# Query copies of VectorE between its scales, and a new order of the first units, in an attention and GEGLU kernel

## The chip, the cores and the metric

The kernel runs on one core of a Trainium2 chip. The metric is the device time of one execution in microseconds (us). Several executions of a kernel are taken beside executions of the kernel before on the same chip; one of them is taken with a profile. The time is about 2 us longer than the span of the profile.

## The reference

Linear attention with cosine weights, then a gated feed-forward block over its output. Eight batches of 576 tokens, eight heads of 64, model width 512, inner width 1536.

```python
def phi(x, c, s):
    r = np.maximum(x, 0.0)
    return np.concatenate([r * c, r * s], axis=-1)
q_p, k_p = phi(q, cos_w, sin_w), phi(k, cos_w, sin_w)
kv = np.einsum('bhsf,bhsd->bhfd', k_p, v);  z = np.sum(k_p, axis=2)
num = np.einsum('bhsf,bhfd->bhsd', q_p, kv)
den = np.einsum('bhsf,bhf->bhs', q_p, z)[..., None] + 1e-06
x = (num / den).transpose(0, 2, 1, 3).reshape(B * S, H * D)
g = x @ w_gate
return (0.5 * g * (1 + erf(g / sqrt(2))) * (x @ w_val)) @ w_out
```

## The kernel before

Only the prologue matters: all that happens before the feed-forward units of the first block run one behind the other. It has two chains that meet in the first unit.

- *Attention.* VectorE and ScalarE scale the keys and queries of batch 0 (`sk`, `sq`), TensorE turns (transposes) the queries (`q_by_pe`) into PSUM, the buffer `ps` that its results go to, and a copy brings them to SBUF, the main on-chip memory (`q_evac`), TensorE makes the kv products (`kv_half`) and the numerators (`numer_mm`), VectorE normalises (`norm`), TensorE turns the result, a copy puts it into `xT` (`x_by_pe`). The 576 tokens are five column tiles x0 to x4 (the last is 64 wide).
- *Weights.* `load_w(j0, j1)` lets GpSimd issue two DMAs, one of gate and one of value weights, that cast from fp32 to bf16. A one-element ScalarE copy that reads the end of `qf` holds the first of them back until the queries have landed.

A feed-forward unit is four gate matmuls, a Gelu on ScalarE, four value matmuls and a product on VectorE. Its arguments are block, weight column, first token, width, gate bank and value bank (a bank is one of the slots of `ps`, its second index; a unit that re-uses a bank has to wait until the bank has been read):

```python
def gv_unit(n, jt, c0, w, gb, vb, mid=()):
    p0 = starts[n] + c0
    for ct in range(CT):
        nc.tensor.matmul(ps[:, gb, 0:w], lhsT=wg_sb[:, ct, jt*128:(jt+1)*128],
                         rhs=xT[:, ct, p0:p0+w], start=(ct == 0), stop=(ct == CT-1))
    gel = rot.tile([128, 512], FP32, name="gel", bufs=3)
    nc.scalar.activation(gel[:, 0:w], ps[:, gb, 0:w], AF.Gelu)
    for f in mid:
        f()
    for ct in range(CT):
        nc.tensor.matmul(ps[:, vb, 0:w], lhsT=wv_sb[:, ct, jt*128:(jt+1)*128], ...)
    nc.vector.tensor_mul(hT[n % 2][:, jt, 64+c0:64+c0+w], gel[:, 0:w], ps[:, vb, 0:w])
```

The prologue (cuts marked):

```python
dummies(22)                     # junk matmuls, meant to warm TensorE's clock
...                             # scales of the keys
for h0 in (0, 4):
    if h0:
        nc.scalar.copy(wg_sb[0:1, 0, 0:1], qf[0:1, 7, NJ, D - 1:D])
        load_w(0, 2)
    for j in range(NJ + 1):
        sq(j, 0, "v", h0, h0 + 4)
        sq(j, 1, "v" if j < 2 else "s", h0, h0 + 4)
    for j in range(NJ):
        q_by_pe(0, j, j, None, h0, h0 + 4)
    dummies(2, 7)
q_evac(0, 0, 0, "s")
cast_v(0, 0, 2, "v"); cast_v(0, 2, 4, "s")
load_w(2, 4)
kv_half(0, 0, 4, None)
cast_v(0, 4, 6, "v"); cast_v(0, 6, 8, "s")
q_evac(0, 1, 1, "v")
...                             # kv, numerators and turn of x0, x1
gv_unit(0, 0, 0, 128, 0, 1);   gv_unit(0, 1, 0, 128, 5, 4)      # tile 0
x_by_pe(0, 1, x1, 0, "s");     x2 = numer(0, 2, 6)
gv_unit(0, 0, 128, 128, 5, 1); gv_unit(0, 1, 128, 128, 0, 4)    # tile 1
q_evac(0, 3, 3, "v");          q_by_pe(0, 4, 2, "s")
x_by_pe(0, 2, x2, 5, "s");     x3 = numer(0, 3, 6)
gv_unit(0, 0, 256, 128, 0, 1); gv_unit(0, 1, 256, 128, 3, 4)
x_by_pe(0, 3, x3, 5, "s");     x4 = numer(0, 4, 6)
gv_unit(0, 2, *A, 0, 1);       gv_unit(0, 3, *A, 3, 4)          # A = (0, 256)
x_by_pe(0, 4, x4, 5, "v")
gv_unit(0, 2, *Bw, 0, 1);      gv_unit(0, 3, *Bw, 3, 4)         # Bw = (256, 320)
gv_unit(0, 0, 384, 192, 0, 1); gv_unit(0, 1, 384, 192, 3, 4)
...
for jt in range(4, 11):         # "the regular units"
    gv_unit(0, jt, *A, 0, 3);  gv_unit(0, jt, *Bw, 1, 2)
```

I call everything up to the first tile's units *the front* and what follows, up to the regular units, *the back*.

## Time and profile before

| | before |
|---|---|
| time, median of 3 runs | 334.81 us (334.25 to 334.89) |
| span of the profile | 332.7 us |
| first gate matmuls / first value matmuls | 18.32 / 19.13 us |
| second tile's gate matmuls | 20.87 us |
| regular units start | 31.66 us |
| from there to the end | 301.0 us |

The page of the kernel before: busy time of the engines with their share of the span, and two rows of its 40 slices in tenths.

```profile
PE 321.7 (97%) x2260; PEld 171.5 (52%) x2260; DVE 177.2 (53%) x394; ACT 149.9 (45%) x275; POOL 21.5 (6%) x39
...
PE   7879999999999999999999999999999999999995
...
PEclk9799999999999999999999999999999999999999
```

TensorE has gaps in the first three slices and at the end only. So the start of the regular units is the number to watch: what the prologue saves, the kernel saves.

The chain of waits of the same profile over the prologue (start, length, what):

```profile
4.88 5.52 DMA qf<-in_q_dram
...
10.92 2.56 POOL wg_sb L292
13.48 5.60 DMA wv_sb<-in_moe_w_val_dram
...
19.13 0.40 PE ps L222 x4
```

The timeline of the same profile, cut to GpSimd's weight issues, some of VectorE's work beside them, and TensorE's milestones (start, length, engine, line, operation; in brackets the idle time before and what ended it):

```profile
10.92 2.57 POOL L292 DMA_DIRECT2D wg_sb<-in_moe_w_gate_dram  x1 [8.20 <-ACT wg_sb L345]
...
11.97 0.87 DVE L132 TENSOR_SCALAR qp<-qf,cos_c 128x256 bf16<-128x256 f32 x3
...
12.76 0.55 DVE L138 CAST vx<-vf 128x640 bf16<-128x640 f32 x1
...
13.48 0.90 POOL L293 DMA_DIRECT2D wv_sb<-in_moe_w_val_dram  x1
...
13.66 0.56 DVE L138 CAST vx<-vf 128x640 bf16<-128x640 f32 x1 [0.35 <-DMA vf<-in_v_dram]
...
18.32 0.64 PE L213 MATMUL ps<-xT,wg_sb 128*128 128x128 bf16 x4
...
19.13 0.40 PE L222 MATMUL ps<-xT,wv_sb 128*128 128x128 bf16 x4 [0.17 <-DMA wv_sb<-in_moe_w_val_dram]
...
20.87 0.38 PE L213 MATMUL ps<-xT,wg_sb 128*128 128x128 bf16 x4 [0.42 <-ACT xT L327]
...
28.15 0.72 PE L213 MATMUL ps<-xT,wg_sb 128*128 128x320 bf16 x4 [0.70 <-DVE xT L329]
...
31.66 0.60 PE L213 MATMUL ps<-xT,wg_sb 128*128 128x256 bf16 x4
```

The first weight issue took 2.57 us; it ended in the first pause of VectorE, between two casts at 13.31 and 13.66. The value weights landed at 19.08, and 0.17 us of TensorE's idle time is put down to them.

### The profile page before, as it was taken

Reading aid. Unit: us, or ns where it says so; the run is one execution under the profiler, and the core shown is the slowest. Engines: PE = TensorE matmul, PEld = TensorE weight load, DVE = VectorE, ACT = ScalarE, POOL = GpSimd, SP = SyncE. Lnnn points to the kernel's source line nnn. Section 1 sums busy time; section 2 is a strip of 40 time slices with the busy share of each in tenths; the row PEclk is TensorE's granted clock in tenths of the full one; section 3 lists DMA queues with packets and bytes.
Section 4 is the critical chain, followed back from the end, with each engine's and each line's share of the span. In section 5 each row is a group of like instructions: output and inputs, shape, how many; then the busy total and the mean of one; then the engine's idle time right before and its main releaser. Section 6 shows DMA issues by size and latency. Waiting matters only on the chain.

```text
span 332.7 us, 5946 instructions
## 1 busy us (share of the span) xinstructions
PE 321.7 (97%) x2260; PEld 171.5 (52%) x2260; DVE 177.2 (53%) x394; ACT 149.9 (45%) x275; POOL 21.5 (6%) x39
## 2 busy tenths in 40 slices
PE   7879999999999999999999999999999999999995
PEld 2567766765445444544454445544454444444443
DVE  5775468776674548454755576457635323222210
ACT  6764468783473237422742265325532322322321
POOL 2550010000100001000100010001000100000000
PEclk9799999999999999999999999999999999999999
DMA  7899998999388965994499439992925121000024
GB/s 239 229 166 206 242 340 264 310 226 359 66 112 231 349 102 95 249 323 119 86 253 333 110 75 203 375 142 54 184 47 76 21 63 34 32 32 33 33 64 95
DMA packets 84380, 54.65 MB, mean 164 GB/s; under 512 B 49408, under 2 KB 79872, under 8 KB 84352
## 3 DMA queue, kind: packets, MB, share of 16 engines
q1 hardware_dynamic: 78128, 49.10, 59.2%
q0 software_dynamic: 5792, 4.72, 9.2%
q10 hardware_dynamic: 432, 0.46, 0.4%
q8 instruction: 17, 0.28, 0.3%
q14 instruction: 11, 0.09, 0.1%
HBM read 37.75 MB, written 9.44 MB: 142 GB/s over the span
## 4 chain that ended last, share of the span: by engine, by line
PE 86%; DVE 4%; DMA 3%; ACT 2%; issue 2%; POOL 1%; SPq 1%; DVEq 0%; POOLq 0%; ACTq 0%
PE ps L245 27%; PE ps L213 26%; PE ps L222 26%; PE ps L167 3%; DVE vx L138 3%; PE ps L151 2%; DMA wv_sb<-in_moe_w_val_dram 2%; DMA qf<-in_q_dram 2%; PE ps L311 1%; PE ps L264 1%; ACT kp L134 1%; POOL wg_sb L292 1%; SPq L78 1%; ACT xT L327 1%; DVE hT L226 0%
## 5 line engine op out<-in xcount | busy, mean ns | idle before, releaser
L226 DVE TENSOR_TENSOR hT<-gel,ps 128x512 bf16<-128x512 f32 (+4 forms) x128 | 77.1, 603 | 130.4 <-PE ps L222 127.5
L213 PE MATMUL ps<-xT,wg_sb 128*128 128x512 bf16 (+5 forms) x512 | 114.4, 346 | 2.1 <-ACT xT L327 1.2
L222 PE MATMUL ps<-xT,wv_sb 128*128 128x512 bf16 (+5 forms) x512 | 114.3, 346 | 0.2 <-DMA wv_sb<-in_moe_w_val_dram 0.2
L218 ACT ACTIVATE gel<-ps 128x512 f32<-128x512 f32 (+4 forms) x128 | 67.8, 531 | 85.1 <-PE ps L213 83.7
L245 PE MATMUL ps<-wo_sb,hT 128*128 128x512 bf16 x420 | 96.2, 379 | 0.0
L222 PEld LDWEIGHTS <-wv_sb 128*128 128x128 bf16 x512 | 48.8, 98 | 45.5 <-DMA wv_sb<-in_moe_w_val_dram 0.3
L213 PEld LDWEIGHTS <-wg_sb 128*128 128x128 bf16 x512 | 46.8, 98 | 41.9 <-issue 2.1
L245 PEld LDWEIGHTS <-hT 128*128 128x128 bf16 x420 | 40.2, 98 | 45.8
L275 ACT COPY o_sb<-ps 128x512 f32<-128x512 f32 x35 | 20.5, 586 | 75.5 <-PE ps L245 72.4
L182 DVE TENSOR_TENSOR xb<-ps,rec 128x512 bf16<-128x512 f32 (+1 forms) x41 | 27.8, 678 | 1.5
L134 ACT ACTIVATE kp<-kf,sin_c 128x512 bf16<-128x512 f32 (+1 forms) x41 | 25.3, 679 | 0.7 <-DMA kf<-in_k_dram 0.7
L132 DVE TENSOR_SCALAR qp<-qf,cos_c 128x512 bf16<-128x512 f32 (+1 forms) x45 | 21.0, 510 | 0.7 <-DMA qf<-in_q_dram 0.7
L167 PEld LDWEIGHTS <-qT 128*128 128x128 bf16 x320 | 15.1, 98 | 9.1 <-issue 1.8
L134 ACT ACTIVATE qp<-qf,sin_c 128x512 bf16<-128x512 f32 (+1 forms) x30 | 18.8, 670 | 0.3 <-DMA qf<-in_q_dram 0.3
L132 DVE TENSOR_SCALAR kp<-kf,cos_c 128x512 bf16<-128x512 f32 (+1 forms) x45 | 18.0, 451 | 1.0 <-DMA kf<-in_k_dram 1.0
L167 PE MATMUL ps<-kv,qT 128*128 128x65 bf16 x320 | 16.8, 193 | 0.6 <-DVE qT L317 0.4
L206 POOL COPY xT<-xr 128x256 bf16<-128x256 bf16 x6 | 2.4, 401 | 205.2 <-DMA xr<-xb 205.2
L151 PEld LDWEIGHTS <-kp 128*128 128x128 bf16 x320 | 11.5, 99 | 3.8 <-issue 2.9
L151 PE MATMUL ps<-vx,kp 128*128 128x65 bf16 x320 | 12.2, 195 | 0.5
L138 DVE CAST vx<-vf 128x1280 bf16<-128x1280 f32 (+1 forms) x14 | 12.1, 892 | 0.3 <-DMA vf<-in_v_dram 0.3
L124 PE MATMUL ps<-junk 128*128 128x512 bf16 x32 | 10.0, 450 | 1.7 <-DVE par_i L101 1.7
L231 POOL COPY hT<-hT 128x768 bf16<-128x768 bf16 x8 | 7.6, 946 | 39.5 <-DVE hT L226 39.5
(53 smaller groups left out, 93.9 us busy)
## 6 DMA issues: line engine op xcount, KB each, us to landing
out_dram<-o_sb SPq DMA_DIRECT2D x38, 128.0 KB, 2.4
qf<-in_q_dram SPq DMA_DIRECT2D x7, 640.0 KB, 6.1
kf<-in_k_dram SPq DMA_DIRECT2D x7, 640.0 KB, 8.1
out_dram<-o_sb SPq DMA_DIRECT2D x16, 256.0 KB, 3.0
vf<-in_v_dram SPq DMA_DIRECT2D x6, 640.0 KB, 9.7
qf<-in_q_dram SPq DMA_DIRECT2D x7, 512.0 KB, 4.8
kf<-in_k_dram SPq DMA_DIRECT2D x7, 512.0 KB, 6.7
vf<-in_v_dram SPq DMA_DIRECT2D x6, 512.0 KB, 8.4
```

Source lines behind the costliest of these rows:

```text
L132: nc.vector.tensor_scalar(d, s, col, 0.0, op0=ALU.mult, op1=ALU.max)
L134: nc.scalar.activation(d, s, AF.Relu, scale=col)
L138: cp(vx[b % 2][:, :, h0:h1, 0:D], vf[:, h0:h1].rearrange("p h j d -> p j h d"))
L151: nc.tensor.matmul(ps[:, bank, (h % 4) * (D + 1):(h % 4 + 1) * (D + 1)], lhsT=kp[:, j, h, :], rhs=vx[b % 2][:, j, h, 0:D + 1], start=(j == ...
L167: nc.tensor.matmul(ps[:, bank + g, (h % 4) * (D + 1):(h % 4 + 1) * (D + 1)], lhsT=qT[b % 2][:, t, h, :], rhs=kv[b % 2][:, h, 0:D + 1], sta ...
L182: nc.vector.tensor_tensor(xb[:, g0:g1], nd[:, :, :, 0:D], rec[:, 0:n, :, None].to_broadcast([128, n, 4, D]), op=ALU.mult,)
L213: nc.tensor.matmul(ps[:, gb, 0:w], lhsT=wg_sb[:, ct, jt * 128:(jt + 1) * 128], rhs=xT[:, ct, p0:p0 + w], start=(ct == 0), stop=(ct == CT - 1),
L218: nc.scalar.activation(gel[:, 0:w], ps[:, gb, 0:w], AF.Gelu)
L222: nc.tensor.matmul(ps[:, vb, 0:w], lhsT=wv_sb[:, ct, jt * 128:(jt + 1) * 128], rhs=xT[:, ct, p0:p0 + w], start=(ct == 0), stop=(ct == CT - 1),
L226: nc.vector.tensor_mul(hT[n % 2][:, jt, 64 + c0:64 + c0 + w], gel[:, 0:w], ps[:, vb, 0:w])
L245: nc.tensor.matmul(ps[:, bank, :], lhsT=hT[n % 2][:, jt, c0:c0 + 128], rhs=wo_sb[:, jt, :], start=(jt == 0), stop=(jt == JT - 1),)
L275: nc.scalar.copy(o_sb, ps[:, bank, :])
```

## The change

Its intent: VectorE copies query turns out of PSUM *between* its scales, so that GpSimd gets to issue the weights; copies, turns and units follow the order in which their inputs arrive; the 192-wide pair of units is split into 128 and 64, so that its first part need not wait for x4. Core of the diff:

```diff
-    dummies(22)
+    dummies(30)
     ...  # scales of the keys as before, then those of the queries' first half (a4), turned
-    (gate of the loads, load_w(0, 2), second half's scales, its turns, dummies(2, 7))
-    q_evac(0, 0, 0, "s")
-    cast_v(0, 0, 2, "v")
-    cast_v(0, 2, 4, "s")
+    nc.scalar.copy(wg_sb[0:1, 0, 0:1], qf[0:1, 7, NJ, D - 1:D])
+    load_w(0, 2)
     load_w(2, 4)
+    q_evac(0, 0, 0, "v", *a4)
+    sq(0, 0, "v", *b4), sq(0, 1, "s", *b4)
+    sq(1, 0, "v", *b4), sq(1, 1, "v", *b4)
+    q_evac(0, 1, 1, "v", *a4)
+    for j in range(2, NJ + 1):
+        sq(j, 0, "v", *b4), sq(j, 1, "s", *b4)
+    ...  # turns of the second half, dummies(1, 7)
+    cast_v(0, 0, 4, "s")
     kv_half(0, 0, 4, None)
     cast_v(0, 4, 6, "v")
     cast_v(0, 6, 8, "s")
-    q_evac(0, 1, 1, "v")
+    q_evac(0, 0, 0, "v", *b4)
+    q_evac(0, 1, 1, "v", *b4)
     ...
     gv_unit(0, 0, 0, 128, 0, 1)
     gv_unit(0, 1, 0, 128, 5, 4)
     x_by_pe(0, 1, x1, 0, "s")
+    q_evac(0, 3, 3, "s", *a4)
     x2 = numer(0, 2, 6)
     gv_unit(0, 0, 128, 128, 5, 1)
     gv_unit(0, 1, 128, 128, 0, 4)
-    q_evac(0, 3, 3, "v")
-    q_by_pe(0, 4, 2, "s")
-    x_by_pe(0, 2, x2, 5, "s")
+    q_evac(0, 3, 3, "s", *b4)
+    x_by_pe(0, 2, x2, 2, "v")
     x3 = numer(0, 3, 6)
-    gv_unit(0, 0, 256, 128, 0, 1)
-    gv_unit(0, 1, 256, 128, 3, 4)
-    x_by_pe(0, 3, x3, 5, "s")
+    gv_unit(0, 2, *A, 5, 1)
+    q_by_pe(0, 4, 3, "s")
+    gv_unit(0, 3, *A, 0, 4)
+    x_by_pe(0, 3, x3, 2, "s")
     x4 = numer(0, 4, 6)
-    gv_unit(0, 2, *A, 0, 1)
-    gv_unit(0, 3, *A, 3, 4)
-    x_by_pe(0, 4, x4, 5, "v")
-    gv_unit(0, 2, *Bw, 0, 1)
-    gv_unit(0, 3, *Bw, 3, 4)
-    gv_unit(0, 0, 384, 192, 0, 1)
-    gv_unit(0, 1, 384, 192, 3, 4)
+    gv_unit(0, 0, 256, 128, 5, 1)
+    gv_unit(0, 1, 256, 128, 0, 4)
+    gv_unit(0, 0, 384, 128, 5, 1)
+    gv_unit(0, 1, 384, 128, 0, 4)
+    x_by_pe(0, 4, x4, 3, "v")
+    gv_unit(0, 2, *Bw, 5, 1)
+    gv_unit(0, 3, *Bw, 0, 4)
+    gv_unit(0, 0, 512, 64, 5, 1)
+    gv_unit(0, 1, 512, 64, 0, 4)
```

More of the change, by code (lines that the diff above doesn't have):

```diff
@@ L335, in sk @@
         scale(K, j, which, eng, *h)
-    dummies(22)
+    a4, b4 = (0, 4), (4, 8)
+    dummies(30)
     for h0 in (0, 4):
@@ L342 @@
             sk(j, 1, "v" if j < 2 else "s", h0, h0 + 4)
-    for h0 in (0, 4):
-        if h0:
-            nc.scalar.copy(wg_sb[0:1, 0, 0:1], qf[0:1, 7, NJ, D - 1:D])
-            load_w(0, 2)
-        for j in range(NJ + 1):
-            sq(j, 0, "v", h0, h0 + 4)
-            sq(j, 1, "v" if j < 2 else "s", h0, h0 + 4)
-        for j in range(NJ):
-            q_by_pe(0, j, j, None, h0, h0 + 4)
-        dummies(2, 7)
-    q_evac(0, 0, 0, "s")
-    cast_v(0, 0, 2, "v")
-    cast_v(0, 2, 4, "s")
-    load_w(2, 4)
+    for j in range(NJ + 1):
+        sq(j, 0, "v", *a4)
+        sq(j, 1, "v" if j < 2 else "s", *a4)
+    for j in range(NJ):
+        q_by_pe(0, j, j, None, *a4)
+    dummies(1, 7)
+    nc.scalar.copy(wg_sb[0:1, 0, 0:1], qf[0:1, 7, NJ, D - 1:D])
+    load_w(0, 2)
+    load_w(2, 4)
+    q_evac(0, 0, 0, "v", *a4)
[4 more added lines that the diff above has]
+        sq(j, 0, "v", *b4), sq(j, 1, "s", *b4)
+    for j in range(NJ):
+        q_by_pe(0, j, j, None, *b4)
+    dummies(1, 7)
+    cast_v(0, 0, 4, "s")
     kv_half(0, 0, 4, None)
@@ L366 @@
     norm(x0, 6, 0, 1)
-    dummies(2, 4)
+    dummies(1, 4)
     numer_mm(0, 0, 6, 1)
     norm(x0, 6, 1, 2)
-    q_evac(0, 2, 2, "s", 0, 4)
+    q_evac(0, 2, 2, "s", *a4)
     dummies(1, 5)
@@ L375 @@
     x1 = numer(0, 1, 6)
-    q_evac(0, 2, 2, "s", 4, 8)
+    q_evac(0, 2, 2, "s", *b4)
     nc.gpsimd.tensor_copy(tiny[0:1, 1:2], x0[0:1, 1, 3, D - 1:D])
```

## The prediction

> **What bounds the kernel now.** TensorE is busy 97% of the 332.7 us span (busy table). After about 31.7 us it has practically no gaps: the windows view gives 268 us busy of 272 between 60 and 332. So only the prologue is left, and the change touches only that. The chain of waits over it: query load to 10.40; a one-element ScalarE gate; GpSimd's issue of the first weight load, 10.92 to 13.48; the first value weights' DMA, landing 19.08; then matmuls broken by waits until 28.15. The regular units (jt = 4) start at 31.66. From 18.3 to 31.66 TensorE is busy 11.04 of 13.36 us: about 2.3 us of gaps, at 19.0, 20.2 to 20.9, 22.6 to 24.0 and 27.4 to 28.15 (timeline).
>
> **The weight issue.** The first GpSimd issue took 2.57 us, later ones 0.75 to 0.76. It ended at 13.48, just after VectorE's unbroken run of scales and a cast (to 13.31). The Trainium skill ("SBUF — State Buffer", the warning on DVE blocking SWDGE DMAs) says that GpSimd can't write descriptors while VectorE runs a 2-port fp32 SBUF operation; this trace agrees (2.57 against 0.75 us). A copy out of PSUM isn't such an operation. The change puts two PSUM query copies of VectorE (half of the 0.68 us for 1024 elements, about 0.4 each) among the second half's scales, at about 10.9 and 12.0. I expect the first issue to end by 11.7 to 12.3 and the second by about 13.4 (before 14.38), so the value weights land about 1 us earlier, near 18.1.
>
> **The attention chain.** This gains less. The first x tile was in SBUF at 18.63, only 0.45 before the weights. The change takes the 1.01 us copy off ScalarE and gives it a cast of about 1.3 us before the first kv product; the second half's scales end 0.4 to 0.5 later on VectorE. Dummies rise from 22 to 30, filling the gap from 8.1 to 9.75 after which the granted clock fell to 0.5 (12 to 14 us); a warmer clock would save some tenths in turns and kv matmuls. I estimate the first x tile at 18.1 to 18.3. The first units, now not waiting for weights, start about 0.5 us earlier.
>
> **The new order.** It moves query copies of tile 3 to ScalarE in halves before they are needed, the x turn of tile 2 to VectorE (0.4 instead of 0.59), and two 256-wide units (0.88 us each, needing only tiles 0 and 1) into the old gap at 22.6 to 24.0. It splits a 192-wide pair into 128 and 64. The total of matmul work is nearly unchanged. New waits are likely: at the fourth tile's units VectorE is in a 1.1 us normalisation, so PSUM comes free late (about 0.6 us), and the 320-wide units still wait for x4 (about 0.6 us). I put the regular units at about 30.7 instead of 31.66.
>
> **Total.** Gain 0.9 us, all on the critical path, since TensorE is full afterwards; the later loads shift with the weight stream. Predicted 333.9 us, 8 in 10 between 333.1 and 334.7; within 2% almost surely.
>
> **What would show it.** First weight issue under 1.5 us; value weights landed near 18; first gate unit near 18 with its value matmuls following directly; no gap over 0.5 us between 22 and 24; jt = 4 gate matmuls starting at 30.2 to 31.2; nothing changed in length after that.
>
> **What would make it wrong.** Scales leaving GpSimd starved between the two copies; earlier weight traffic delaying the value loads (kv product late); the clock throttling later, on real matmuls instead of on turns; the new VectorE order holding up the x4 turn so that all gain is returned before 31 us. Or all the gaps close, and the gain is 2 us.

## The result, and the profile after

The changed kernel took 334.74 us (median of 4 runs, 334.50 to 335.33) beside 334.53 us of the kernel before (4 runs, 333.85 to 334.89). The ratio is 1.0011, with a 95% interval from 0.9988 to 1.0034. A ratio is the mean time of one kernel's runs over that of the other's in the same rounds, so it isn't quite the ratio of the medians. The change shows no gain here, and the median lies just above the predicted range.

The timeline of the changed kernel, cut in the same way:

```profile
11.08 0.42 DVE L317 COPY qT<-ps 128x512 bf16<-128x512 bf16 x1
...
11.18 0.90 POOL L292 DMA_DIRECT2D wg_sb<-in_moe_w_gate_dram  x1 [8.46 <-ACT wg_sb L350]
...
12.07 0.76 POOL L293 DMA_DIRECT2D wv_sb<-in_moe_w_val_dram  x1
...
17.71 0.64 PE L213 MATMUL ps<-xT,wg_sb 128*128 128x128 bf16 x4
...
18.18 0.39 PE L222 MATMUL ps<-xT,wv_sb 128*128 128x128 bf16 x4
...
20.16 0.38 PE L213 MATMUL ps<-xT,wg_sb 128*128 128x128 bf16 x4 [0.42 <-ACT xT L327]
...
21.84 0.30 PE L167 MATMUL ps<-kv,qT 128*128 128x65 bf16 x4 [0.27 <-ACT qT L317]
...
26.61 0.38 PE L222 MATMUL ps<-xT,wv_sb 128*128 128x128 bf16 x4 [0.49 <-DVE hT L226]
...
28.24 0.72 PE L213 MATMUL ps<-xT,wg_sb 128*128 128x320 bf16 x4 [0.58 <-DVE xT L329]
...
31.23 0.28 PE L222 MATMUL ps<-xT,wv_sb 128*128 128x64 bf16 x4 [0.30 <-DVE hT L226]
31.35 0.60 PE L213 MATMUL ps<-xT,wg_sb 128*128 128x256 bf16 x4
```

The front did what was hoped: the first issue takes 0.90 us, the value weights land at 16.7 (12.07 plus 4.6, the DMA view's time to landing), the first value matmuls wait for nothing and start 0.95 us earlier, the second tile's gate matmuls 0.71 us earlier. But the regular units start only 0.31 us earlier. From the second tile's gate to the regular units the back takes 11.19 us, where before it took 10.79. Three waits stand out: at 26.61 and 31.23 for products of VectorE, and at 28.24 for VectorE's copy of x4. Only the first two are new in kind: the old back waits for x4's copy too, 0.70 us at 28.15. A smaller wait, at 21.84, is for a query copy. From 31.35 to the end it is 301.0 us, as before.

VectorE's timeline in that stretch:

```profile
24.83 0.42 DVE L226 TENSOR_TENSOR hT<-gel,ps 128x256 bf16<-128x256 f32 x1 [1.19 <-ACT gel L218]
25.16 0.16 DVE L179 TENSOR_SCALAR den<-ps 128x8 f32<-128x8 f32 x1
...
25.66 0.69 DVE L182 TENSOR_TENSOR xb<-ps,rec 128x512 bf16<-128x512 f32 x1
26.27 0.47 DVE L226 TENSOR_TENSOR hT<-gel,ps 128x128 bf16<-128x128 f32 x2
...
27.76 0.42 DVE L329 COPY xT<-ps 128x256 bf16<-128x256 bf16 x1
```

VectorE waited 1.19 us for a Gelu that stood behind a 1.01 us query copy on ScalarE. It then normalised x4, and only then made the products of tile 2, which free the PSUM banks of the next two units. It copied x4 last.

### The profile page after: what moved, and what is told of

Its sections match the earlier page's. It is cut to its first block, busy times and chain, and to the rows that moved or that the text cites. A ratio compares the mean times of both kernels' runs of the same rounds, so it can differ in the third digit from the quotient of the medians.

```text
span 332.4 us, 6000 instructions
## 1 busy us (share of the span) xinstructions
PE 322.4 (97%) x2281; PEld 171.3 (52%) x2281; DVE 177.2 (53%) x397; ACT 150.3 (45%) x278; POOL 19.7 (6%) x39
## 4 chain that ended last, share of the span: by engine, by line
PE 89%; DVE 5%; ACT 2%; issue 1%; DMA 1%; DVEq 0%; ACTq 0%
PE ps L245 27%; PE ps L213 26%; PE ps L222 26%; PE ps L167 3%; PE ps L124 3%; DVE vx L138 3%; PE ps L151 2%; PE ps L311 1%; PE ps L264 1%; ACT kp L134 1%; DMA out_dram<-o_sb 1%; DVE hT L226 1%; PE ps L325 1%; ACT gel L218 0%; DVE xb L182 0%
## 5 line engine op out<-in xcount | busy, mean ns | idle before, releaser
L226 DVE TENSOR_TENSOR hT<-gel,ps 128x512 bf16<-128x512 f32 (+5 forms) x130 | 77.0, 596 | 131.3 <-PE ps L222 128.1
L218 ACT ACTIVATE gel<-ps 128x512 f32<-128x512 f32 (+5 forms) x130 | 68.2, 525 | 84.7 <-PE ps L213 83.4
L275 ACT COPY o_sb<-ps 128x512 f32<-128x512 f32 x35 | 20.5, 585 | 75.9 <-PE ps L245 72.8
L124 PE MATMUL ps<-junk 128*128 128x512 bf16 x37 | 11.4, 451 | 1.7 <-DVE par_i L101 1.7
L138 DVE CAST vx<-vf 128x1280 bf16<-128x1280 f32 (+1 forms) x13 | 11.7, 934 | 0.3 <-DMA vf<-in_v_dram 0.3
```

The lines of the kernel that those rows point to most:

```text
L124: nc.tensor.matmul(ps[:, bank, :], lhsT=junk[:, 0:128], rhs=junk, start=True, stop=True)
L138: cp(vx[b % 2][:, :, h0:h1, 0:D], vf[:, h0:h1].rearrange("p h j d -> p j h d"))
L226: nc.vector.tensor_mul(hT[n % 2][:, jt, 64 + c0:64 + c0 + w], gel[:, 0:w], ps[:, vb, 0:w])
```

## The experiments

Two questions. Where did the front's gain go (theory T1: to the fourth tile in the new back)? And what does the front really gain? The second came up after the first experiments, when the kernel before showed two kinds of runs.

All traces in one table. "Gate" and "value" are the first gate and value matmuls, "tile 1" the second tile's gate matmuls, "regular" the regular units; "back" is regular minus tile 1. The time is that of the profiled run.

| run | front | back's order | time | gate | value | tile 1 | regular | back |
|---|---|---|---|---|---|---|---|---|
| before | old | old | 334.75 | 18.32 | 19.13 | 20.87 | 31.66 | 10.79 |
| after | new | new | 334.50 | 17.71 | 18.18 | 20.16 | 31.35 | 11.19 |
| e0_again | new | new | 334.65 | 17.93 | 18.41 | 20.39 | 31.57 | 11.18 |
| e1_front | new | old | 334.58 | 18.28 | 18.76 | 20.74 | 31.53 | 10.79 |
| e2_back | old | new | 335.37 | 17.29 | 19.37 | 21.11 | 32.30 | 11.19 |
| e3_banks | new | new, banks | 333.95 | 18.29 | 18.76 | 20.74 | 30.86 | 10.12 |
| e4_before_again | old | old | 334.39 | 17.50 | 18.81 | 20.55 | 31.34 | 10.79 |
| e5_before_30 | old, 30 dummies | old | 335.00 | 17.49 | 19.41 | 21.15 | 31.94 | 10.79 |
| e6_after_22 | new, 22 dummies | new | 334.53 | 17.82 | 18.29 | 20.27 | 31.45 | 11.18 |
| e8_holes_only | old, copies between | old | 334.84 | 18.52 | 19.00 | 20.97 | 31.76 | 10.79 |
| e9_late_weights | new, weights late | new | 336.93 | 17.65 | 19.95 | 22.08 | 33.87 | 11.79 |
| e10_order | new | rewritten | 332.21 | 17.70 | 18.18 | 20.16 | 29.07 | 8.91 |
| e11_late_dummies | as e9, busy | new | 336.16 | 17.96 | 20.16 | 21.89 | 33.07 | 11.18 |
| e12_before_look | old | old | 335.14 | 17.46 | 19.52 | 21.27 | 32.05 | 10.78 |
| e13_before_look | old | old | 338.07 | 17.62 | 20.43 | 22.99 | 35.00 | 12.01 |

(e7_no_holes isn't listed, its profile is of another state.)

### Front and back apart (one chip, 5 rounds)

**e0_again**: the changed kernel, no edit.

> The changed kernel again, unaltered, with more rounds. In the first trace its regular units (first 256-wide gate matmul of jt = 4) started at 31.35 us against 31.66 before, and the rest took 301.0 us in both. Theory T1 (the front of the change gains 0.6 to 0.7 us, its new order of units gives some 0.4 back at the fourth tile): this run starts them at 31.1 to 31.6, time 0.1 to 0.5 us under before. Rival T2 (the start of the dummies' full clock and the landing of the first loads differ from run to run by as much as the gain): the start moves by more than 0.4 us against the first trace, and the times of single runs spread by about 1 us.

Measured: 334.75 us (6 runs, 334.55 to 335.26). The regular units start at 31.57, in the expected band; the back is 11.18 again, so it is a property of the code. The rival T2, that runs differ by as much as the gain, is not borne out by this trace: the start moved by 0.22 us, the runs spread by 0.7. It isn't refuted either: over all traces with this front and early weights, tile 1 starts between 20.16 and 20.74 (see e1 and e8). The kernel before, in the same rounds on this chip, had a median of 336.75 (11 runs from 334.20 to 337.82). The ratio is 0.9951 (0.9922 to 0.998): in these rounds the change *is* faster, by half a per cent, and by more than T1 expected.

**e1_front**: lines of the changed kernel up to the first units, lines of the kernel before from there on.

> The change's front alone (dummies, query copies among the scales, early weight issue), with the old order of units after x1. T1: the gate matmuls of the second tile start near 20.2 (before 20.87) and the regular units near 31.0, so about 0.7 us under before. If instead the old order gives the front's gain back too (it waits for weights or copies that did not move), they start at 31.4 or later.

Measured: 334.45 us (333.94 to 334.65), 0.30 under e0_again in the same rounds. The back is 10.79, exactly the old one. The start of 31.53 missed my "near 31.0", because tile 1 began at 20.74 in this trace: the front differs from run to run by up to 0.6 us. The landing of the queries isn't the reason here, for the first weight issue starts at 11.17, and in the first trace at 11.18. But VectorE's last scale ends at 14.42 and not at 13.69; e8 shows why. The time was 2.3 us under the median of the kernel before in these rounds, not 0.7, because most of that kernel's runs were slow ones. So backs are compared by their length, not by their end.

**e2_back**: the reverse.

> The change's new order of units alone, behind the old front. T1: the stretch from the second tile's gate to the regular units is 11.2 us (as after) and not 10.8 (as before), so the regular units start near 32.05, 0.4 us later than before, time 0.3 to 0.5 us over before. If the new order is good by itself and the front is what disappoints, they start before 31.5.

Measured: 336.69 us (335.37 to 336.88), ratio to the kernel before 0.9997 (0.9966 to 1.0028), back 11.19. So the time was not 0.3 to 0.5 over before: that part missed, and 0.40 us can't be seen beside runs that spread by 3.6. By the length of the back T1 holds: with either front, the new order is 0.40 us longer than the old. This trace also shows what the first one hid. The first gate matmuls start at 17.29, and the value matmuls then wait for their weights until 19.37, 1.44 us of it idle.

**e3_banks**: the changed kernel, other bank numbers.

```diff
-    gv_unit(0, 0, 384, 128, 5, 1)
-    gv_unit(0, 1, 384, 128, 0, 4)
-    x_by_pe(0, 4, x4, 3, "v")
+    gv_unit(0, 0, 384, 128, 5, 3)
+    gv_unit(0, 1, 384, 128, 0, 2)
+    x_by_pe(0, 4, x4, 1, "v")
...
-    gv_unit(0, 0, 512, 64, 5, 1)
-    gv_unit(0, 1, 512, 64, 0, 4)
+    gv_unit(0, 0, 512, 64, 6, 5)
+    gv_unit(0, 1, 512, 64, 7, 2)
```

> The changed kernel with other PSUM banks for the two units of the fourth tile, the x4 turn and the two 64-wide units; order unchanged. T1 says that the waits at 25.9 to 26.6 and 30.6 to 31.2 are for PSUM banks that VectorE frees late. Then both go away (about 1.2 us of wait), the x4 copy still waits for VectorE, and the regular units start at 30.2 to 30.6, time 0.7 to 1.1 us under the changed kernel. If the waits are for something else (gel buffers, VectorE's order), they stay and the start is within 0.2 us of the changed kernel's.

Measured: 333.71 us (333.39 to 334.24), 1.04 under e0_again in the same rounds. The back is 10.12, 1.06 shorter; the two bank waits are gone, the wait for x4's copy is not. TensorE's timeline of e3_banks:

```profile
28.21 0.72 PE L213 MATMUL ps<-xT,wg_sb 128*128 128x320 bf16 x4 [0.63 <-DVE xT L329]
...
30.75 0.28 PE L222 MATMUL ps<-xT,wv_sb 128*128 128x64 bf16 x4
30.86 0.60 PE L213 MATMUL ps<-xT,wg_sb 128*128 128x256 bf16 x4
```

The number of a bank alone was worth a microsecond. (The start of 30.86 is outside my band by 0.26, again because tile 1 began late.)

### Why the kernel before has two kinds of runs

**e4_before_again** (no edit), **e5_before_30** and **e6_after_22** (the numbers of dummies exchanged):

> The kernel before, unaltered, for a second trace: on the last chip its runs spread from 334.2 to 337.8 us, while kernels with the new front stayed within 0.8 us. Theory T3 (clock): TensorE idles from 8.1 to 9.75 us and the granted clock falls to 0.5 at a moment that differs from run to run; a slow run shows that clock over the kv products, numerators or first units, and those late. Rival T4 (weights): a slow run has the clock at 1.0 but the first value weights landing well after 19.1 us, because GpSimd's first issue ends later or its DMA takes longer.

> The kernel before with 30 dummies at the start in place of 22, nothing else. T3: no idle of TensorE at 8 to 10 us, the clock stays at 1.0, and the times lie within 1 us of each other near 334.5. T4: the times spread as those of before; first weight issue 2.5 us and value weights at 19.1 or later as before.

> The changed kernel with 22 dummies in place of 30. T3: its times spread by 1.5 us or more, with a clock below 1 in its trace between 11 and 16 us, median 1 us over the changed kernel's 334.75. T4: its times stay within 0.8 us, median within 0.4 us of 334.75, first weight issue under 1.1 us.

Measured: e4 334.82 (334.18 to 336.11), e5 336.52 (335.00 to 336.71), e6 334.46 (334.26 to 334.63). T3, that TensorE's idle time before its first turns makes runs slow, falls: with 30 dummies the kernel before is no steadier, and with 22 the changed one is as steady as with 30. What differs between them is the weights, as T4 has it: first issue 2.52 and 2.25 us in e4 and e5, 0.90 in e6. But T4 also expected slow runs to keep a clock of 1.0, and they don't: the four runs of e4 and e5 over 335.7 us have a mean clock of 0.994 or 0.995.

**e7_no_holes**: the changed kernel, the two copies moved behind the scales.

```diff
-    q_evac(0, 0, 0, "v", *a4)
     sq(0, 0, "v", *b4), sq(0, 1, "s", *b4)
     sq(1, 0, "v", *b4), sq(1, 1, "v", *b4)
-    q_evac(0, 1, 1, "v", *a4)
     for j in range(2, NJ + 1):
         sq(j, 0, "v", *b4), sq(j, 1, "s", *b4)
+    q_evac(0, 0, 0, "v", *a4)
+    q_evac(0, 1, 1, "v", *a4)
```

> The changed kernel with the two query copies of VectorE moved from between the scales to after them, so that VectorE reads SBUF alone from 9.2 to about 13 us. If GpSimd's issue waits for such a copy, the first weight issue takes about 2.0 us or more (0.9 to 1.0 with the copies between), it ends only when the scales end (near 13.0), and the first value matmul waits for its weights until about 19; time 0.3 to 1 us over the changed kernel's. If the issue is short anyway (under 1.2 us), the copies' place has nothing to do with it and the earlier gate or lesser load is the reason.

The issue in the timeline of e7_no_holes:

```profile
11.07 2.03 POOL L292 DMA_DIRECT2D wg_sb<-in_moe_w_gate_dram  x1 [8.34 <-ACT wg_sb L350]
```

The issue takes 2.03 us and ends at 13.09, after the last scale (12.79), as expected. The profiled execution was a slow one of an odd kind: 483 us, with a mean granted clock of 0.659 over the whole of it. VectorE's and GpSimd's times show no trace of that clock (a scale took 0.35 us and GpSimd's second issue 0.75, as ever), so the issue can be read from it, but TensorE's times can't, and whether the value matmuls wait for weights stays open there. (The value weights landed at 18.1, by the DMA view 5.0 us after their issue at 13.09; I had expected 19.) The other three runs were 334.57 to 335.06, their median 0.44 us over that of e6_after_22 in the same rounds (which has 22 dummies): in the expected range, though small beside the spread.

**e8_holes_only**: the kernel before with those two half copies between the scales, and nothing else.

```diff
         for j in range(NJ + 1):
+            if h0 and j in (0, 2):
+                q_evac(0, j // 2, j // 2, "v", 0, 4)
             sq(j, 0, "v", h0, h0 + 4)
...
-    q_evac(0, 0, 0, "s")
+    q_evac(0, 0, 0, "s", 4, 8)
...
-    q_evac(0, 1, 1, "v")
+    q_evac(0, 1, 1, "v", 4, 8)
```

> The kernel before with one thing of the change: VectorE copies the first half of the query turns 0 and 1 between the second half's scales (ScalarE and VectorE copy the other halves where they copied all). Theory T4 (GpSimd's issue is starved by VectorE, the first value weights then land last and at a time that differs by run): the first issue takes 0.9 to 1.2 us and not 2.5, the weights are there before the first gate matmuls end, the times stay within 1 us of each other, and the median is 333.9 to 334.6. Rival (the order of the weights or of the copies elsewhere in the new front is what steadies it): the issue is short, but the times spread by 2 us like before's.

The issue and two of VectorE's scales in the timeline of e8_holes_only:

```profile
10.92 0.99 POOL L292 DMA_DIRECT2D wg_sb<-in_moe_w_gate_dram  x1 [8.19 <-ACT wg_sb L345]
...
11.24 0.34 DVE L132 TENSOR_SCALAR qp<-qf,cos_c 128x256 bf16<-128x256 f32 x1
...
12.17 0.60 DVE L132 TENSOR_SCALAR qp<-qf,sin_c 128x256 bf16<-128x256 f32 x1
```

Two copies of 0.4 us from PSUM bring the issue from 2.5 us to 0.99: this part of the change is shown, both by adding and by taking it away. But the time is 335.00 (334.84 to 337.04): over the expected band, with a spread of 2.2 us, which is the rival's outcome. The weights now land at 16.8, two microseconds before they are needed; in exchange VectorE's scales and casts end later, and the first gate matmuls start at 18.52 where other traces of the old front have them near 17.5. The bound only moved to the attention chain.

The copies are not the whole price. Four of VectorE's scales beside GpSimd's issues took 0.49 to 0.60 us instead of 0.35, and each ended about 0.1 us after an issue did: once GpSimd gets in, VectorE waits in its turn. The traces with copies between the scales and early weights have two to four such long scales, those without the copies none (e9 and e11, with late weights, have none and one). This is also what makes the new front uneven: in its six traces the last scale ends between 13.69 (after, e10) and 14.43 (e3), and the first gate matmuls follow in the same order, from 17.70 to 18.29. I take it that the new front needs the rest of the change too, which hands a cast to ScalarE; that was not tested by itself.

Two of the six runs (335.95 and 337.04) were slow although the profiled one had early weights, and neither was profiled. The record says this much: the first has a span of 332.7 us, like the fast ones, so its loss lies outside the span; the second has a mean clock of 0.990. What lowered that clock stays open.

**e9_late_weights**: the changed kernel with the gate of the loads, and the loads, behind the last scale.

```diff
-    nc.scalar.copy(wg_sb[0:1, 0, 0:1], qf[0:1, 7, NJ, D - 1:D])
-    load_w(0, 2)
-    load_w(2, 4)
     ...
         sq(j, 0, "v", *b4), sq(j, 1, "s", *b4)
+    nc.scalar.copy(wg_sb[0:1, 0, 0:1], qf[0:1, 7, NJ, D - 1:D])
+    load_w(0, 2)
+    load_w(2, 4)
```

> The changed kernel with the gate of the weight loads moved behind ScalarE's last scale, so that the loads are issued near 13.1 and 13.9 us, as late as in the kernel before, with everything else new. T4: the first value matmul waits for weights until 19.2 or later, the times spread by 1.5 us or more, median 335.3 to 337. Rival (something else in the old front makes it late and uneven): the times stay within 0.8 us and the median within 0.5 us of 334.75.

Measured: 336.92 (335.52 to 337.57). Late weights make the changed kernel as slow as the slow runs of the kernel before. (They are a little later here: the value issue starts at 13.89, in the kernel before at 13.48.) The windows of e9_late_weights (stretch, length, then busy time and instructions of PE, PEld, DVE, ACT and POOL, granted clock, DMA share, GB/s) show a second cost:

```profile
19.00:20.00 1.00, 0.05 (x1) 0.05 (x2) 0.00 (x0) 0.00 (x0) 1.00 (x2) 1.00 1.41 176
20.00:21.00 1.00, 1.00 (x15) 1.00 (x16) 0.29 (x1) 0.28 (x1) 1.00 (x2) 0.73 1.39 183
21.00:22.00 1.00, 0.84 (x12) 0.73 (x11) 0.41 (x2) 0.56 (x2) 1.00 (x2) 0.50 1.34 191
22.00:23.00 1.00, 0.92 (x10) 0.92 (x10) 0.93 (x3) 0.79 (x3) 0.03 (x1) 0.50 1.26 207
23.00:24.00 1.00, 1.00 (x13) 1.00 (x12) 0.30 (x2) 0.45 (x2) 0.00 (x0) 0.56 1.24 206
```

TensorE sat idle for 1.66 us before its value weights came at 19.95; at about 20.5 the clock fell to half. The back became 0.6 us longer. The six runs agree: five have a mean clock of 0.993 to 0.995 and took 336.79 to 337.57 us, and the one with a clock of 1.0 took 335.52.

**e11_late_dummies**: e9_late_weights with junk matmuls in that wait.

```diff
-    gv_unit(0, 0, 0, 128, 0, 1)
+    gv_unit(0, 0, 0, 128, 0, 1, mid=(lambda: dummies(8, 1),))
```

> The kernel of e9_late_weights (336.9 us; clock 0.5 from 20.4 to 23.5 us) with eight junk matmuls, about 1.7 us, between the first unit's gate and value matmuls, where TensorE sat idle for its weights. Theory T5 (the wait costs twice: by itself and by the clock that falls after it): the clock stays at 1.0 from 18 to 26 us, the stretch from the second tile's gate to the regular units is 11.2 us again (11.8 in e9), and the median is 335.6 to 336.3, 0.7 us or more under e9. Rival (the wait alone makes these runs slow; the low clock hides behind other waits): the median stays within 0.3 us of 336.9.

Measured: 336.19 (335.76 to 336.56), 0.73 under e9, with the clock at 1.0 throughout and the back at 11.18 again, although the value matmuls start 0.21 later than in e9. All six runs have a mean clock of 0.998 or more. T5 holds: late weights cost twice, by the wait and by the clock that falls after it. (e9 and e11 ran in different rounds.)

**e12_before_look** and **e13_before_look**: the kernel before, for a trace of a slow run.

> The kernel before, for a trace of a slow run (15 of its 37 runs so far were over 335.7 us). T5: if it is over 335.7 us, the clock is under 0.8 for 2 us or more between 17 and 26 us, or the first value matmul starts after 19.8 us; if it is near 334.5, neither. Rival (slow runs come from the end of the kernel or the middle): the regular units start by 31.8 us and the time from there to the end is over 301.5 us.

> As e12_before_look, a second chance of a slow run of the kernel before, with the same two expectations.

The second was slow: 338.07 us. Its chain of waits:

```profile
11.38 2.54 POOL wg_sb L292
13.92 6.46 DMA wv_sb<-in_moe_w_val_dram
...
20.43 0.61 PE ps L222 x4
```

And its windows:

```profile
18.00:19.00 1.00, 0.26 (x2) 0.08 (x1) 0.89 (x2) 0.60 (x2) 1.00 (x3) 1.00 1.07 128
19.00:20.00 1.00, 0.00 (x0) 0.00 (x0) 0.00 (x0) 0.00 (x0) 1.00 (x2) 0.87 1.18 133
20.00:21.00 1.00, 0.57 (x6) 0.57 (x7) 0.00 (x0) 0.00 (x0) 1.00 (x2) 0.50 1.37 185
...
26.00:27.00 1.00, 0.58 (x10) 0.47 (x9) 0.35 (x2) 1.00 (x2) 0.00 (x0) 0.72 1.24 200
```

Everything that e9 did on purpose happened here by itself. The queries landed 0.5 us late, the starved issue took 2.55 us, the DMA 6.46 us where the first trace has 5.60. (Why this DMA takes longer in some runs was not tested.) TensorE waited 2.17 us for weights, its clock fell at about 19.7 and came back at about 26.6, and the regular units started at 35.00, 3.3 us later than in the first trace. From there to the end it is 301.0 us as always. e12, at 335.14, waited 1.42 us and kept its clock in that stretch.

### Can both be beaten?

**e10_order**: the changed front, a back that follows from T1.

```diff
     x2 = numer(0, 2, 6)
+    q_by_pe(0, 4, 2, None)                 # into the wait for x1
     gv_unit(0, 0, 128, 128, 5, 1); gv_unit(0, 1, 128, 128, 0, 4)
     q_evac(0, 3, 3, "s", *b4)
-    x_by_pe(0, 2, x2, 2, "v")
+    x_by_pe(0, 2, x2, 5, "v")
+    q_evac(0, 4, 2, "s")
     x3 = numer(0, 3, 6)
-    gv_unit(0, 2, *A, 5, 1)
-    q_by_pe(0, 4, 3, "s")
-    gv_unit(0, 3, *A, 0, 4)
-    x_by_pe(0, 3, x3, 2, "s")
-    x4 = numer(0, 4, 6)
-    (the 128-wide units with banks 5, 1 and 0, 4 twice, then x4's turn)
+    gv_unit(0, 2, *A, 3, 1)
+    x4 = new_xb()
+    gv_unit(0, 3, *A, 0, 4, mid=(          # between gate and value matmuls
+        lambda: x_by_pe(0, 3, x3, 2, "s"),
+        lambda: numer_mm(0, 4, 6, 0), lambda: numer_mm(0, 4, 6, 1),
+        lambda: norm(x4, 6, 0, 2)))
+    gv_unit(0, 0, 256, 128, 5, 1); gv_unit(0, 1, 256, 128, 3, 2)
+    x_by_pe(0, 4, x4, 0, "v")
+    gv_unit(0, 0, 384, 128, 6, 7); gv_unit(0, 1, 384, 128, 5, 4)
+    gv_unit(0, 2, *Bw, 3, 1);      gv_unit(0, 3, *Bw, 0, 2)
+    gv_unit(0, 0, 512, 64, 6, 7);  gv_unit(0, 1, 512, 64, 5, 4)
```

> The changed front with a new order of the units up to the regular ones: the turn of query tile 4 goes into the wait for x1, x3's turn and the numerators of tile 4 go between gate and value of unit 3, so that VectorE normalises x4 before the gated product of that unit; each unit has its own PSUM banks. Theory T1 (in the changed kernel the gain is lost at the fourth tile, to VectorE's normalisation of x4 and banks that it frees late): no wait of TensorE over 0.15 us between 21 us and the regular units, the stretch from the second tile's gate to the regular units takes 8.8 to 9.4 us (after 11.2, before 10.8), time 332.2 to 333.2. If the stretch stays over 10 us, the fourth tile's waits came from something that I have not named.

Measured: 332.42 us (331.99 to 332.94), ratio to the kernel before 0.9914 (0.9875 to 0.9952). The changed kernel had 334.75 in e0_again, on a chip of the same number but in other rounds. The back is 8.91 us, 2.28 shorter than in the changed kernel; the difference of the medians is 2.33. TensorE's timeline of e10_order:

```profile
20.16 0.38 PE L213 MATMUL ps<-xT,wg_sb 128*128 128x128 bf16 x4
...
26.43 0.71 PE L213 MATMUL ps<-xT,wg_sb 128*128 128x320 bf16 x4
...
28.95 0.28 PE L222 MATMUL ps<-xT,wv_sb 128*128 128x64 bf16 x4
29.07 0.60 PE L213 MATMUL ps<-xT,wg_sb 128*128 128x256 bf16 x4
```

VectorE's timeline of e10_order:

```profile
24.05 0.17 DVE L179 TENSOR_SCALAR den<-ps 128x8 f32<-128x8 f32 x1 [0.42 <-PE ps L167]
...
25.16 0.81 DVE L226 TENSOR_TENSOR hT<-gel,ps 128x256 bf16<-128x256 f32 x3
25.88 0.42 DVE L329 COPY xT<-ps 128x256 bf16<-128x256 bf16 x1
```

VectorE begins to normalise x4 at 24.05 (25.16 in the changed kernel) and has copied it by 26.3 (28.2). All matmuls of x4's tile start without a wait. One bracket over 0.15 us remains after 21 us, 0.27 before a numerator at 21.83, so "no wait over 0.15" was missed there. The work of TensorE is the same as in the changed kernel; only its order and the banks differ. Part of the shorter back is work that left it: the turns of query tile 4 (0.45 us in the changed kernel, from 22.85 to 23.30) now fill the wait before tile 1. The shares of this, of the banks and of the earlier normalisation were not measured apart, except for the banks in e3.

## Why the prediction was wrong

- **The weight issue: right.** Expected to end by 11.7 to 12.3, it ended at 12.08; the second, expected by 13.4, ended at 12.83. The cause is shown: with the copies 0.90 to 0.99 us (seven traces: six of the new front, and e8), without them 2.03 (e7) to 2.61 (the old front). The page "SBUF — State Buffer" of the Trainium skill, in its warning on VectorE blocking GpSimd's DMAs, names the mechanism, and these runs agree.
- **The first units start "about 0.5 us earlier": right for these two traces** (gate 0.61, value 0.95), but for the gate that was luck: it compares with a trace whose attention was late (see below).
- **"New waits are likely … about 0.6 us": right.** They were 0.49 for a bank and 0.58 for x4.
- **The step that failed is the gain of the new order, in "I put the regular units at about 30.7 instead of 31.66".** They started at 31.35. My sum gave the new order a gain of about 0.4 us beside the front's 0.5. Measured apart, the order *costs* 0.40 (11.19 against 10.79, with either front). The two waits that I saw were not too low. I missed two others: 0.30 at 31.23, for the bank of the last 64-wide unit, and 0.27 at 21.84, where the numerators of tile 3 wait for ScalarE's second half of a query copy. And VectorE's copy of x4 starts 7.60 us after tile 1's gate, in the old back 6.81: so "the new VectorE order holding up the x4 turn", which I had put under what would make it wrong, came about. e3 shows that other banks take off 1.06 us, e10 that with an earlier query turn and an earlier normalisation of x4 it is 2.28.
- **Why equal brackets make unequal backs.** The brackets of TensorE's matmuls add up to 1.64 us in the old back and in the new. But a stop costs more than its bracket. Four 128-wide matmuls are listed as 0.38 to 0.40 us long, and without a wait the next ones start after 0.22; the other 0.17 us are lost at each stop. The old back has three stops, the new one five (one, before the numerators at 24.57, too short for a bracket). Counted from start to start, my estimate from the two timelines is 2.2 us lost against 2.5.
- **"This gains less. The first x tile was in SBUF at 18.63, only 0.45 before the weights" was read from one trace, and this trace was not typical.** Its clock was at half from about 11.5 to 15 us, and its attention was late, which hid the wait for weights. Five other traces with the old front and no copies between the scales (e2, e4, e5, e12, e13) have attention ready at 17.3 to 17.6 and value matmuls at 18.8 to 20.4: TensorE sat idle for 0.67 to 2.17 us of that, by the brackets. In these five the clock stayed at 1.0 until the value weights were waited for, so I take the low clock for the reason of the late attention. Weights bound that front, and by more than I took. The new front's attention is not faster, gate matmuls at 17.7 to 18.3; its weights are.
- **What the first comparison couldn't show.** Of the 50 runs of the kernel before in all rounds, on several chips, 30 are under 335.7 us with a mean of 334.57, and 20 are over it with a mean of 336.87. (335.7 is my cut; the times alone show no clear gap.) The mean clock, which the record has for 46 of them, parts them better: all 20 slow runs have 0.990 to 0.995, and 23 of the other 26 have 0.997 or more. The other three, 334.69 to 335.69 us, have 0.993 or 0.994, and so has the profile of the kernel before, whose clock fell ahead of the units. The changed kernel's ten runs lie between 334.50 and 335.33, and none of the 32 runs with the new front and early weights (after, e0, e1, e3, e6, e10) has a clock under 0.997. If two in five runs are slow, and each by itself, four runs are all fast with a chance of 0.6 to the fourth power, 13%; that is what the first comparison drew. Against fast runs the change gains nothing, against slow ones two microseconds. A lower clock goes with every slow run. That late weights lowered it is shown for e13, the one slow run of the kernel before that was profiled, and by e9 and e11; for the others it is argued.

The range from 333.1 to 334.7 was also narrow for a kernel of which I had three times and one trace.

## What to carry to other kernels

When VectorE works in SBUF without a pause, a DMA that GpSimd issues waits for it; a PSUM copy placed among its operations lets the issue through, in under 1 us here instead of over 2, but then VectorE's scales beside the issue take up to 0.60 us instead of 0.35. Before you reckon with a gain upstream, follow the last engine downstream: here in-order VectorE work and re-used PSUM banks gave the gain back. Other bank numbers were worth 1.06 us, and together with an earlier turn and an earlier normalisation 2.3 us. Look at several traces and many times before you call a wait short, above all where a wait on TensorE can lower its clock for the matmuls behind it.

## What the Trainium skill lacked or had wrong

- "SBUF — State Buffer", the warning on VectorE blocking GpSimd's DMAs: it speaks of one operation. Here an issue didn't get done between back-to-back scales either: it took 2.57 us and ended 0.17 us after a run of scales and a cast without pauses. The cure that the warning names, issuing from another queue, isn't the only one: two PSUM copies of 0.4 us among the scales bring the issue to 0.90 to 0.99 us. Their price is VectorE's, whose scales beside the issues take up to 0.60 us instead of 0.35.
- "TensorE: Matmul & The Clock Gate", "Why this matters for your kernels", asks for no idle gaps over about 3 us. That row alone would let all the waits here pass. Waits of 1.66 us (e9) and 2.17 us (e13), among sparse small matmuls, were enough for half clock, and half clock followed one of 1.65 us in the kernel before (up to 9.75); waits of 1.28, 1.42 and 1.44 us (e5, e12, e2) weren't enough. With one trace of each this shows no threshold. Its window of 3413 ns (Part 1) agrees: from the slices, the clock was at half for 3.42 us in e9 and for 6.8 us in e13.
- The same page, Part 1, puts the penalty of the ramp, the cold matmuls at the start, at under 1% of a typical span. A fall in the middle of a kernel, which that figure isn't about, is as small here (0.73 us of 336 between e9 and e11), but in kernels tuned to tenths of a per cent it decides the comparison.
- No page that I read explains an execution like that of e7: 483 us, with a granted clock of 1.0 up to about 7.4 us and of 0.65 from there to the end, on a single core whose other runs took 335 us.
